# Attention with mixed heads and routed experts: scores of two pairs of heads per visit, one visit for all products with v, neighbouring columns in the second mixing

## The chip, the core and the metric

The kernel runs on one core of one Trainium2 chip. The metric is the device time of one execution in microseconds (us). A core has five engines that work at the same time, each through its own instructions in a fixed order: TensorE (PE, matrix products, with weight loads listed as PEld), VectorE (DVE), ScalarE (ACT), GpSimd (POOL) and SyncE (SP, which here only issues transfers). They wait for one another through semaphores. PE writes its results to PSUM, a small memory of eight banks per partition, and DVE or ACT copy them out to the main on-chip memory.

## What is computed

Attention over 8 batches, 12 heads, 448 positions and 64 values per head, with two mixings of the heads (before and after the softmax), and then a layer of 8 experts of which each row uses one:

```python
scores = scale * np.matmul(q, k.transpose(0, 1, 3, 2))
scores = np.einsum('bhij,hg->bgij', scores, w_pre)
scores = scores - np.max(scores, axis=-1, keepdims=True)
attn = np.exp(scores)
attn = attn / (np.sum(attn, axis=-1, keepdims=True) + 1e-09)
attn = np.einsum('bhij,hg->bgij', attn, w_post)
x = np.matmul(attn, v)                      # then heads side by side: 3584 x 768
...
logits = x @ w_gate
expert_idx = np.argmax(logits, axis=1)
...
for e in range(E):
    h = np.maximum(xe @ w1[e], 0.0)
    out[mask] = gate_w[mask, None] * (h @ w2[e])
```

All data are float32.

## The kernel before

The attention works on 32 tiles T: four to a batch, three of 120 queries and one of 88 (`it` is the tile's number in its batch). The 12 heads are 6 pairs c; a pair's two heads lie in the two halves of the partitions.

For each tile, `qk` (L203) is called once per pair. It makes the scores of the pair with six matrix products, three for each head (q and k are split into a high and a low part, and high x high, high x low and low x high are added). The two heads use the upper and the lower half of the array's rows at the same time and write two PSUM banks, the tile `bs` (bank_s). ACT then copies both banks to `si` (L215). There is one such pair of banks, so the next visit waits until ACT has emptied it. I call one call of `qk` a **scores visit**.

SP's transfers (`relayout`, L227) then gather 10 queries x 12 heads onto partitions, into one of four `sb` tiles. Such a **block** holds two groups of at most 10 queries; a tile of 120 has 6 blocks, the tile of 88 has 5, the last of them with one group. Group n of N holds the queries n, n+N, n+2N, ... (`queries`, L61). For every block stand one after the other:

- `mix` (L234), the **first mixing**: a product of full array width per group (L241, into `bm`; a float32 product is run as two passes, which the profile lists as two MATMUL), the negative maximum on DVE (L242), the exponential with its sum on ACT (L243).
- `weigh` (L248): one over the sum on DVE (L251, L253), and the mixing weights scaled by it, `wp`, on POOL (L256).
- `post` (L260), the **second mixing**, one step later: four products of full width per group (L267, into `bp`), which also turn the block so that keys lie on partitions; DVE copies them to `pt` (L271). Since a group's queries lie N apart, this copy writes every N-th column of `pt` (N is 12, or 9 in the short tile).

When all blocks of a tile are done, `av` (L278), the **products with v**, runs in two halves g of three pairs: 24 products each (L286), the two heads of a pair side by side in two halves of the array's columns, into one bank `ba`; DVE copies it to `xt` (L289). `rows` (L293) turns the result back into rows and multiplies by the router's weights, in two parts (L301, into a bank `bx`; ACT L303, DVE L304). `dispatch` (L313) finds each row's expert and place: small DVE rows, two tiny products (L328, L329, into `bx`), and an indirect transfer that POOL issues (L346).

`split_q` (L115) makes the high and the low part of q, on ACT (L121) and POOL (L122).

What runs when is a list of steps u, one for each block: `at(u, priority, what)` in L386 to L407 puts a call into a step, and within a step calls go by priority. Scores of a tile were spread over the steps from 8 to 4 ahead of its first block, the second mixing stands one step behind its first mixing, and the products with v, the rows and the dispatch some steps behind the tile's last block. A scheduler then sets the final order on each engine, so that it may differ from the list by some places; on the chip every engine keeps this order.

Behind the attention comes the expert stage (from L421), which the change doesn't touch.

Of the kernel before, what the change touches and what calls it, by code (L numbers as in the profile page):

```python
# [23 lines left out]
P = 128  # L24
IT = 120
# [15 lines left out]
def attn_moe_kernel(ctx, tc, qT, kT, v, w_pre, w_post, w_gate, w1, w2, out):  # L41
# [19 lines left out]
    def queries(T, s, c):  # L61
        N, n = geom[T][4], 2 * s + c
        return slice(n, n + N * (geom[T][3][s][c] - 1) + 1, N)

# [16 lines left out]
    ps_a = att.enter_context(tc.tile_pool(name="ps_a", bufs=1, space=PSUM))  # L81
    ps_x = att.enter_context(tc.tile_pool(name="ps_x", bufs=1, space=PSUM))

    bank_s = ps_s.tile([P, 2, 512], F32, name="bs")
    bank_m = [ps_m.tile([P, 512], F32, name=f"bm{n}") for n in range(2)]
    bank_p = [ps_p.tile([JC, 512], F32, name=f"bp{n}") for n in range(2)]
    bank_a = ps_a.tile([P, 3, IT], F32, name="ba")
    bank_x = [ps_x.tile([P, 512], F32, name="bx"), bank_s[:, 0, :]]
# [26 lines left out]
    def split_q(T, part):  # L115
        ni = geom[T][2]
        if part == 0:
# [3 lines left out]
        nc.scalar.copy(out=qh[:, cs, :ni], in_=QR[T][:, cs, :ni])  # L121
        nc.gpsimd.tensor_sub(out=ql[:, cs, :ni], in0=QR[T][:, cs, :ni],  # L122
                             in1=qh[:, cs, :ni].bitcast(F32))
# [79 lines left out]
    def qk(T, c):  # L203
        b, it, ni = geom[T][:3]
        if c == 0:
            SI[T] = si_p.tile([IT, H, S], F32, name="si")
        kh, kl = KK[b, c]
        qh, ql = QQ[T]

        for n, (qx, kx) in enumerate(((qh, kh), (qh, kl), (ql, kh))):  # L210
            for r in range(2):
                hs = slice(r * D, (r + 1) * D)
                nc.tensor.matmul(out=bank_s[:ni, r, :S], lhsT=qx[hs, c, :ni], rhs=kx[hs, :],  # L213
                                 start=(n == 0), stop=(n == 2))
        nc.scalar.copy(out=SI[T][:ni, 2 * c:2 * c + 2, :], in_=bank_s[:ni, :, :S])  # L215
        m = (it - 2) * NPAIR + c - NPAIR + 2
        if b + 1 < B:
            if 0 <= m < NPAIR:
                load_k(b + 1, m)
            if 1 <= m <= NPAIR:  # L220
                split_k(b + 1, m - 1)
# [5 lines left out]
    def relayout(T, s):  # L227
        sb = sbs[nsb["n"] % len(sbs)]
        nsb["n"] += 1
        for c, nq in enumerate(geom[T][3][s]):  # L230
            nc.sync.dma_start(out=sb[R0:R0 + nq * H, c, :], in_=SI[T][queries(T, s, c)])
# [43 lines left out]
    PA = {}  # L275


    def av(T, g):  # L278
        b, it, ni = geom[T][:3]
        if g == 0:  # L280
            XT[T] = x_p.tile([P, NPAIR, IT], F32, name="xt")
        for p in range(3):
            for c in range(NJ):
                for r in range(2):
# [390 lines left out]
```

## Time and profile before

| what | value |
|---|---|
| time, median of 3 runs | 1592.8 us (1588.83 to 1593.34) |
| the profiled execution | 1589.2 us |
| its span, first to last instruction | 1587.0 us |
| PE: busy, share of the span | 1511.4 us, 95% |
| DVE, ACT, POOL: share of the span | 56%, 42%, 27% |

The profile shows one execution. Its page lists groups of instructions by source line, with how often they ran, their busy time and the mean duration of one. The trace behind the page answers further questions: the busy time of each engine in a stretch of time, who waited for whom, and the instructions of an engine in the order of time. In such a timeline a row has the start (us from the span's beginning), the time until the last of the row's instructions ended, the engine, the line, the operation, output<-inputs, their shapes, and how many instructions were merged. Since PE overlaps the end of one product with the start of the next, the distance from start to start tells what an instruction costs, and the busy time doesn't.

PE starts in the attention at 7.5 us and with the expert stage at 1026 us.

### The profile page before, as it was taken

Reading aid. Unit: us, or ns where it says so; the run is one execution under the profiler, and the core shown is the slowest. Engines: PE = TensorE matmul, PEld = TensorE weight load, DVE = VectorE, ACT = ScalarE, POOL = GpSimd, SP = SyncE. Lnnn points to the kernel's source line nnn. Section 1 sums busy time; section 2 is a strip of 40 time slices with the busy share of each in tenths; the row PEclk is TensorE's granted clock in tenths of the full one; section 3 lists DMA queues with packets and bytes.
Section 4 is the critical chain, followed back from the end, with each engine's and each line's share of the span. In section 5 each row is a group of like instructions: output and inputs, shape, how many; then the busy total and the mean of one; then the engine's idle time right before and its main releaser. Section 6 shows DMA issues by size and latency. Waiting matters only on the chain. (4 is left out here: it accounts for less than half of the span.)

```text
span 1587.0 us, 29453 instructions
## 1 busy us (share of the span) xinstructions
PE 1511.4 (95%) x11056; PEld 1190.4 (75%) x11056; DVE 892.5 (56%) x2003; ACT 661.5 (42%) x1424; POOL 429.8 (27%) x595
## 2 busy tenths in 40 slices
PE   5999999999999999999999999499999999999996
PEld 2767777777777767777777776498988898997986
DVE  1666767767766776776776768435243333434320
ACT  4554454454454454554445444134233222333320
POOL 5443342342352342343233222112012020201100
PEclk9999999999999999999999999799999999999998
DMA  7443343342443433433423224345162433426210
GB/s 204 138 135 107 128 143 107 125 151 97 137 137 101 149 124 108 150 118 118 143 102 112 88 98 138 97 134 198 40 226 84 155 136 103 162 84 216 97 50 37
DMA packets 114465, 197.51 MB, mean 124 GB/s; under 512 B 39746, under 2 KB 88914, under 8 KB 114308
## 3 DMA queue, kind: packets, MB, share of 16 engines
q1 hardware_dynamic: 107200, 171.51, 33.4%
q0 software_dynamic: 6064, 23.86, 4.1%
q8 instruction: 100, 1.64, 0.4%
q14 instruction: 57, 0.47, 0.1%
q10 hardware_dynamic: 1044, 0.04, 0.0%
HBM read 96.01 MB, written 23.06 MB: 75 GB/s over the span
## 5 line engine op out<-in xcount | busy, mean ns | idle before, releaser
L243 ACT ACTIVATE et<-bm,st 124x448 f32<-124x448 f32 x360 | 225.7, 631 | 424.1 <-DVE st L242 332.8
L271 DVE COPY pt<-bp 112x480 f32<-112x480 f32 x360 | 344.3, 1011 | 47.8 <-PE bp L267 47.1
L256 POOL TENSOR_SCALAR wp<-Wpost,st 124x120 f32<-124x120 f32 x360 | 208.1, 589 | 566.5 <-DVE st L253 531.3
L267 PEld LDWEIGHTS bp<-wp,et 124*112 124x112 f32 x2880 | 309.5, 177 | 60.3 <-issue 51.8
L267 PE MATMUL bp<-wp,et 124*112 124x120 f32 x2880 | 345.8, 272 | 4.6 <-POOL wp L256 3.9
L241 PE MATMUL bm<-sb,Wpre 124*124 124x448 f32 x720 | 305.4, 546 | 0.0
L242 DVE TENSOR_REDUCE st<-bm 124x1 f32<-124x448 f32 x360 | 218.4, 614 | 25.1 <-PE bm L241 17.1
L215 ACT COPY si<-bs 120x896 f32<-120x896 f32 (+1 forms) x192 | 172.7, 899 | 33.1 <-PE bs L213 33.0
L286 PEld LDWEIGHTS ba<-pt,vt 112*64 112x64 f32 x3072 | 151.7, 138 | 32.3 <-issue 22.1
L241 PEld LDWEIGHTS bm<-sb,Wpre 124*124 124x124 f32 x720 | 120.8, 187 | 68.4 <-issue 62.5
L286 PE MATMUL ba<-pt,vt 112*64 112x120 f32 (+1 forms) x3072 | 169.0, 263 | 1.5 <-DVE m L320 1.0
L531 POOL DMA_INDIRECT out<-y,ti x30 | 33.4, 1113 | 464.2 <-ACT xh L458 338.4
L503 PE MATMUL pm_h<-xh,ah 128*128 128x512 f32 (+1 forms) x384 | 148.1, 386 | 1.9 <-ACTq L555 0.7
L503 PE MATMUL pm_h<-xl,ah 128*128 128x512 f32 (+1 forms) x384 | 147.5, 384 | 0.0
L503 PE MATMUL pm_h<-xh,al 128*128 128x512 f32 (+1 forms) x384 | 147.4, 384 | 0.0
L213 PEld LDWEIGHTS bs<-kh,qh 64*120 64x120 f32 (+1 forms) x384 | 34.0, 174 | 135.6 <-issue 98.2
L522 PE MATMUL pm_y<-bh,hh 128*128 128x384 f32 x480 | 127.9, 343 | 0.0
L522 PE MATMUL pm_y<-bl,hh 128*128 128x384 f32 x480 | 123.6, 336 | 0.0
L507 DVE SCALAR_TENSOR_TENSOR hl<-pm_h,hh 128x512 fp32r<-128x512 f32 (+1 forms) x64 | 42.1, 657 | 141.2 <-ACT hh L506 141.2
L522 PE MATMUL pm_y<-bh,hl 128*128 128x384 f32 x480 | 121.1, 336 | 0.0
L213 PE MATMUL bs<-kh,qh 64*120 64x448 f32 (+1 forms) x384 | 90.4, 467 | 24.0 <-ACT si L215 15.1
L527 DVE TENSOR_SCALAR y<-pm_y,tb 128x384 f32<-128x384 f32 x30 | 18.4, 614 | 159.9 <-PE pm_y L522 159.9
(102 smaller groups left out, 1756.2 us busy)
## 6 DMA issues: line engine op xcount, KB each, us to landing
sb<-si SPq DMA_DIRECT2D x344, 210.0 KB
wraw<-in_w SPq DMA_DIRECT2D x48, 512.0 KB
wraw<-in_w SPq DMA_DIRECT2D x64, 384.0 KB
kr<-in_kT SPq DMA_DIRECT2D x48, 224.0 KB
vt<-in_v SPq DMA_DIRECT2D x8, 1344.0 KB
qr<-in_qT SPq DMA_DIRECT2D x48, 180.0 KB
XD<-xr SPq DMA_DIRECT2D x24, 360.0 KB
sb<-si SPq DMA_DIRECT2D x16, 189.0 KB
```

Of the source, the lines that this page charges most:

```text
L213: nc.tensor.matmul(out=bank_s[:ni, r, :S], lhsT=qx[hs, c, :ni], rhs=kx[hs, :], start=(n == 0), stop=(n == 2))
L215: nc.scalar.copy(out=SI[T][:ni, 2 * c:2 * c + 2, :], in_=bank_s[:ni, :, :S])
L241: nc.tensor.matmul(out=bm, lhsT=Wpre[:R1, :], rhs=sb[:R1, c, :], start=True, stop=True)
L242: nc.vector.reduce_max(out=st[:R1, 0, c:c + 1], in_=bm, axis=AX.X, negate=True)
L243: nc.scalar.activation(out=et[:R1, c, :], in_=bm, func=AF.Exp, bias=st[:R1, 0, c:c + 1], scale=1.0, accum_out=st[:R1, 1, c:c + 1])
L256: nc.gpsimd.tensor_scalar(out=wp[:R1, c, :], in0=Wpost[:R1], scalar1=st[:R1, 2, c:c + 1], scalar2=None, op0=ALU.mult)
L267: nc.tensor.matmul(out=pp[:, c * IT:(c + 1) * IT], lhsT=et[:R1, n, c * JC:(c + 1) * JC], rhs=wp[:R1, n, :], start=True, stop=True)
L271: nc.vector.tensor_copy(out=PT[T][:, :, :, queries(T, s, n)].rearrange("p c h i -> p (c h) i"), in_=bank_p[n][:, :NJ * IT].rearrange("p (x ...
L286: nc.tensor.matmul(out=bank_a[r * D:(r + 1) * D, p, :ni], lhsT=VV[b][:, c, h * D:(h + 1) * D], rhs=PT[T][:, c, h, :ni], start=(c == 0), st ...
L503: nc.tensor.matmul(out=ph[:, :n], lhsT=wx[:, fs], rhs=xx[:, kt, :n], start=(m == 0), stop=(m == 3 * NK1 - 1))
L507: nc.vector.scalar_tensor_tensor(out=hl[:, ft, :n], in0=ph[:, :n], scalar=0.0, in1=hh[:, ft, :n].bitcast(F32), op0=ALU.max, op1=ALU.subtract)
L522: nc.tensor.matmul(out=py[g][:, :384], lhsT=hx[:, kt, ts], rhs=wx[:, g * 384:(g + 1) * 384], start=(n == 0), stop=(n == 3 * NK2 - 1))
```

## The change

Five things are changed, all of them in the attention.

1. **Scores of two pairs per visit.** `qk(T, g)` makes pairs 2g and 2g + 1, one into each of two pairs of banks (`bank_s` is now a list of two tiles of two banks); then ACT copies both. Visits stand at the steps 8, 6 and 4 ahead of the tile's first block (7, 5, 3 for the first tile of a batch and 7, 6, 4 for the second: `QSTEP`).
2. **All products with v in one visit.** `av(T)` makes both halves, one in the first bank of each of the two score tiles; the two copies stand behind.
3. **The banks `ba` and `bx` are gone.** `rows` writes the first bank of the one and of the other score tile, `dispatch` the second bank of the first. So these four banks serve the scores, the products with v, the row projection and the dispatch in turn.
4. **Neighbouring columns.** `queries` now gives a group a run of neighbouring columns of `pt`. To match, `split_q` writes the queries of q in another order, so that rows n, n+N, ... of the scores hold neighbouring queries; `relayout` reads the same stepped rows as before (`parts`). The stepped access is thus in `split_q`'s outputs, no longer in the copy to `pt`. The short tile's split takes two instructions each where one did, since its groups have two sizes.
5. **Steps of the tail.** `rows` (both parts) stands w = 2 steps behind `av`, `dispatch` 2 further, all with priority 6, behind the first and ahead of the second mixing of the step; before, the halves of `av` and `rows` were spread over the next tile.

```diff
-    def queries(T, s, c):
+    def parts(T, s, c):
         N, n = geom[T][4], 2 * s + c
         return slice(n, n + N * (geom[T][3][s][c] - 1) + 1, N)
+
+    def queries(T, s, c):
+        nq = sum(geom[T][3], [])
+        i0 = sum(nq[:2 * s + c])
+        return slice(i0, i0 + nq[2 * s + c])
...
-    bank_s = ps_s.tile([P, 2, 512], F32, name="bs")
+    bank_s = [ps_s.tile([P, 2, 512], F32, name=f"bs{n}") for n in range(2)]
...
-    bank_a = ps_a.tile([P, 3, IT], F32, name="ba")
-    bank_x = [ps_x.tile([P, 512], F32, name="bx"), bank_s[:, 0, :]]
...
-        nc.scalar.copy(out=qh[:, cs, :ni], in_=QR[T][:, cs, :ni])
-        nc.gpsimd.tensor_sub(out=ql[:, cs, :ni], in0=QR[T][:, cs, :ni],
-                             in1=qh[:, cs, :ni].bitcast(F32))
+        i0 = 0
+        for k in sorted(set(nq), reverse=True):
+            n0, n1 = nq.index(k), nq.index(k) + nq.count(k)
+            src = QR[T][:, cs, i0:i0 + k * (n1 - n0)].rearrange("p c (n i) -> p c n i", i=k)
+            hi, lo = (q[:, cs, :N * k].rearrange("p c (i n) -> p c n i", n=N)[:, :, n0:n1, :]
+                      for q in (qh, ql))
+            nc.scalar.copy(out=hi, in_=src)
+            nc.gpsimd.tensor_sub(out=lo, in0=src, in1=hi.bitcast(F32))
+            i0 += k * (n1 - n0)
...
+        for c in (2 * g, 2 * g + 1):
+            kh, kl = KK[b, c]
+            for n, (qx, kx) in enumerate(((qh, kh), (qh, kl), (ql, kh))):
+                for r in range(2):
+                    hs = slice(r * D, (r + 1) * D)
+                    nc.tensor.matmul(out=bank_s[c % 2][:ni, r, :S], lhsT=qx[hs, c, :ni],
+                                     rhs=kx[hs, :], start=(n == 0), stop=(n == 2))
+        for c in (2 * g, 2 * g + 1):
+            nc.scalar.copy(out=SI[T][:ni, 2 * c:2 * c + 2, :], in_=bank_s[c % 2][:ni, :, :S])
...
+        for g in range(2):
+            pa = bank_s[g][:, 0, :3 * IT].rearrange("p (c i) -> p c i", i=IT)
+            for p in range(3):
+                for c in range(NJ):
+                    for r in range(2):
+                        h = 2 * (3 * g + p) + r
+                        nc.tensor.matmul(out=pa[r * D:(r + 1) * D, p, :ni],
...
-        px = bank_x[part] if T == NTILE - 1 else bank_x[0]
+        px = bank_s[part][:, 0, :]
...
-        pr = bank_x[0]
+        pr = bank_s[0][:, 1, :]
...
+    QSTEP = {0: (7, 5, 3), 1: (7, 6, 4)}
...
-        for c in range(NPAIR):
-            at(max(u0 - QLEAD + c * 5 // 6, -1), 3, qk, T, c)
+        for g in range(3):
+            at(max(u0 - QSTEP.get(it, (8, 6, 4))[g], -1), 3, qk, T, g)
...
-        w = len(geom[T + 1][3]) - 1 if T + 1 < NTILE else 0
-        for g in range(2):
-            at(ua + g * w // 2, 6, av, T, g)
-            at(ua + g * w // 2 + 1, 9, rows, T, g)
-        at(ua + w // 2 + 2, 9, dispatch, T)
+        w = 2 if T + 1 < NTILE else 1
+        at(ua, 6, av, T)
+        for part in range(2):
+            at(ua + w, 6, rows, T, part)
+        at(ua + 2 * w, 6, dispatch, T)
```

How this changes the order on PE shows in two places. The rows below give line, operation, output<-inputs (bm, bp: banks of the first and second mixing; ba, bs, bx: of products with v, scores, rows), shape, and how many alike follow each other. In the changed kernel the lines are L225 for the scores, L255 and L281 for the mixings, L299 for the products with v, L316 for the rows, L343 and L344 for the dispatch; bs_101 and bs_102 are the two score tiles.

The first place is on PE in the first batch, where a tile of 120 queries gets its products with v. Before:

```order
L241 MATMUL bm_109<-sb_181,Wpre 124x448
L213 MATMUL bs<-kh,qh 120x448 x2
L213 MATMUL bs<-kl,qh 120x448 x2
L213 MATMUL bs<-kh,ql 120x448 x2
L286 MATMUL ba<-pt,vt 64x120 x9
L213 MATMUL bs<-kh,qh 120x448 x2
L213 MATMUL bs<-kl,qh 120x448 x2
L213 MATMUL bs<-kh,ql 120x448 x2
L286 MATMUL ba<-pt,vt 64x120 x15
L267 MATMUL bp_110<-wp,et 112x120 x4
L267 MATMUL bp_111<-wp,et 112x120 x4
```

A scores visit stands ahead of the half of the products with v, and another one within it. In the changed kernel, on PE in such steps, there is one stretch of products with v, and a scores visit in the step behind it:

```order
L255 MATMUL bm_104<-sb_176,Wpre 124x448
L299 MATMUL bs_101<-pt,vt 64x120 x24
L299 MATMUL bs_102<-pt,vt 64x120 x24
L281 MATMUL bp_105<-wp,et 112x120 x4
L281 MATMUL bp_106<-wp,et 112x120 x4
L255 MATMUL bm_103<-sb_173,Wpre 124x448
L255 MATMUL bm_104<-sb_173,Wpre 124x448
```

Two halves and the scores between them have become one run of 48, with full-width mixings on both sides.

The second place is on PE around a dispatch at the boundary of the first two batches, behind the one-group block of the short tile. Before:

```order
L241 MATMUL bm_109<-sb_183,Wpre 124x448
L213 MATMUL bs<-kh,qh 120x448 x2
L213 MATMUL bs<-kl,qh 120x448 x2
L213 MATMUL bs<-kh,ql 120x448 x2
L267 MATMUL bp_110<-wp,et 112x120 x4
L328 LDWEIGHTS tri
L328 MATMUL bx<-ohb,tri 120x8
L329 LDWEIGHTS ones
L329 MATMUL bx<-ohb,ones 128x8
L241 MATMUL bm_108<-sb_180,Wpre 124x448
```

In the changed kernel, on PE at that boundary:

```order
L255 MATMUL bm_104<-sb_176,Wpre 124x448
L225 MATMUL bs_101<-kh,qh 120x448 x2
L225 MATMUL bs_101<-kl,qh 120x448 x2
L225 MATMUL bs_101<-kh,ql 120x448 x2
L225 MATMUL bs_102<-kh,qh 120x448 x2
L225 MATMUL bs_102<-kl,qh 120x448 x2
L225 MATMUL bs_102<-kh,ql 120x448 x2
L343 LDWEIGHTS tri
L343 MATMUL bs_101<-ohb,tri 120x8
L344 LDWEIGHTS ones
L344 MATMUL bs_101<-ohb,ones 128x8
L281 MATMUL bp_105<-wp,et 112x120 x4
```

The dispatch's products have moved from behind the second mixing to straight behind the scores, and write the tile bs_101, which those scores have just filled and which ACT copies out.

More of the change, by code (lines that the diff above doesn't have):

```diff
@@ L80, in attn_moe_kernel @@
     ps_p = att.enter_context(tc.tile_pool(name="ps_p", bufs=1, space=PSUM))
-    ps_a = att.enter_context(tc.tile_pool(name="ps_a", bufs=1, space=PSUM))
-    ps_x = att.enter_context(tc.tile_pool(name="ps_x", bufs=1, space=PSUM))
-    bank_s = ps_s.tile([P, 2, 512], F32, name="bs")
+    bank_s = [ps_s.tile([P, 2, 512], F32, name=f"bs{n}") for n in range(2)]
     bank_m = [ps_m.tile([P, 512], F32, name=f"bm{n}") for n in range(2)]
     bank_p = [ps_p.tile([JC, 512], F32, name=f"bp{n}") for n in range(2)]
-    bank_a = ps_a.tile([P, 3, IT], F32, name="ba")
-    bank_x = [ps_x.tile([P, 512], F32, name="bx"), bank_s[:, 0, :]]
     KR, KK, QR, QQ, VV, SI, SB, EE, PT, XT = ({} for _ in range(10))
@@ L115, in split_q @@
     def split_q(T, part):
-        ni = geom[T][2]
+        N = geom[T][4]
+        nq = sum(geom[T][3], [])
         if part == 0:
@@ L200, in attn_moe_kernel, with qk @@
                         in_=none.unsqueeze(1).to_broadcast([P, 8, ROWS // P // 8, 2]))
-    def qk(T, c):
+    def qk(T, g):
         b, it, ni = geom[T][:3]
-        if c == 0:
+        if g == 0:
             SI[T] = si_p.tile([IT, H, S], F32, name="si")
-        kh, kl = KK[b, c]
         qh, ql = QQ[T]
[L210 to L221, printed above, removed]
+        for c in (2 * g, 2 * g + 1):
[7 more added lines that the diff above has]
+            nc.scalar.copy(out=SI[T][:ni, 2 * c:2 * c + 2, :], in_=bank_s[c % 2][:ni, :, :S])
+            m = (it - 2) * NPAIR + c - NPAIR + 2
+            if b + 1 < B:
+                if 0 <= m < NPAIR:
+                    load_k(b + 1, m)
+                if 1 <= m <= NPAIR:
+                    split_k(b + 1, m - 1)
     nsb = {"n": 0}
@@ L230, in relayout @@
         for c, nq in enumerate(geom[T][3][s]):
-            nc.sync.dma_start(out=sb[R0:R0 + nq * H, c, :], in_=SI[T][queries(T, s, c)])
+            nc.sync.dma_start(out=sb[R0:R0 + nq * H, c, :], in_=SI[T][parts(T, s, c)])
         SB[T, s] = sb
@@ L273, in post, with av @@
                 in_=bank_p[n][:, :NJ * IT].rearrange("p (x i) -> p x i", i=IB)[:, :, :nq])
-    PA = {}
-    def av(T, g):
+    def av(T):
         b, it, ni = geom[T][:3]
[L280 to L284, printed above, removed]
-                    h = 2 * (3 * g + p) + r
-                    nc.tensor.matmul(out=bank_a[r * D:(r + 1) * D, p, :ni],
-                                     lhsT=VV[b][:, c, h * D:(h + 1) * D],
-                                     rhs=PT[T][:, c, h, :ni], start=(c == 0), stop=(c == NJ - 1))
-        nc.vector.tensor_copy(out=XT[T][:, 3 * g:3 * g + 3, :ni], in_=bank_a[:, :, :ni])
+        XT[T] = x_p.tile([P, NPAIR, IT], F32, name="xt")
+        for g in range(2):
[5 more added lines that the diff above has]
+                        nc.tensor.matmul(out=pa[r * D:(r + 1) * D, p, :ni],
+                                         lhsT=VV[b][:, c, h * D:(h + 1) * D],
+                                         rhs=PT[T][:, c, h, :ni], start=(c == 0), stop=(c == NJ - 1))
+        for g in range(2):
+            pa = bank_s[g][:, 0, :3 * IT].rearrange("p (c i) -> p c i", i=IT)
+            nc.vector.tensor_copy(out=XT[T][:, 3 * g:3 * g + 3, :ni], in_=pa[:, :, :ni])
     XR, LG = {}, {}
```

## The prediction

> **What bounds the kernel now.** First the page's top line, then the windows view for the attention stage (stretch, length, busy time and instructions of PE, PEld, DVE, ACT, POOL, then granted clock, DMA share, GB/s), then the two longest of PE's waits in that stage (sum, times, longest).
>
> ```profile
> span 1587.0 us, 29453 instructions
> 40.00:1000.00 960.00, 949.11 (x8078) 686.70 (x8074) 678.83 (x1661) 471.43 (x1122) 334.73 (x488) 1.00 0.38 122
> PE bs L213 <- ACT si L215: 4.8, 15, 0.6
> PE bp L267 <- POOL wp L256: 3.9, 3, 1.8
> ```
>
> Between 40 and 1000 us PE is busy for 949.1 of 960.0 us at the full granted clock, and its two longest waits come to 8.7 us in all. DVE has 71% of that stretch and ACT 49%. So PE's own row of instructions is the clock of this stage; the change doesn't touch the expert stage behind it. A saving must therefore come out of the distance from start to start on PE. Busy time doesn't show that, because a fill or a drain counts as busy. So I read PE's timeline (start, duration, instruction, count).
>
> ```profile
> 479.06 1.67 PE L241 MATMUL bm<-sb,Wpre 124*124 124x448 f32 x4
> 480.66 0.46 PE L213 MATMUL bs<-kh,qh 64*120 64x448 f32 x2
> 480.96 0.36 PE L213 MATMUL bs<-kl,qh 64*120 64x448 f32 x2
> 481.16 0.36 PE L213 MATMUL bs<-kh,ql 64*120 64x448 f32 x2
> 481.45 1.90 PE L267 MATMUL bp<-wp,et 124*112 124x120 f32 x16
> 483.18 0.86 PE L301 MATMUL bx<-xg,xt 128*120 128x136 f32 x6
> ...
> 985.03 1.67 PE L241 MATMUL bm<-sb,Wpre 124*124 124x448 f32 x4
> 986.54 1.80 PE L267 MATMUL bp<-wp,et 124*112 124x120 f32 x16
> 988.18 0.86 PE L301 MATMUL bx<-xg,xt 128*120 128x136 f32 x6
> ```
>
> The two stretches hold the same first and second mixing (L241, L267), once with a scores visit (L213) between them and once without. L241 takes 1.60 us to the scores (479.06 to 480.66), but 1.51 us straight to L267. L267 takes 1.73 us behind the scores, 1.64 us without them. Inside the visit one step is 0.20 us (480.96 to 481.16), while the whole visit takes 0.79 us where three such steps would be 0.60. Going from full-width products to half-array products and back thus costs 0.09 in front, 0.19 inside and 0.09 behind: **0.37 us for a visit that stands alone**, whatever it computes.
>
> The products with v (L286) have the same kind of price, and are dearer where a scores visit cuts a half in two:
>
> ```profile
> 494.68 2.68 PE L286 MATMUL ba<-pt,vt 112*64 112x120 f32 x48
> 494.94 2.42 PE L286 MATMUL ba<-pt,vt 112*64 112x120 f32 x44
> 497.09 0.27 PE L286 MATMUL ba<-pt,vt 112*64 112x120 f32 x2
> 497.29 1.89 PE L267 MATMUL bp<-wp,et 124*112 124x120 f32 x16
> ...
> 505.28 1.24 PE L286 MATMUL ba<-pt,vt 112*64 112x120 f32 x18
> 506.81 0.47 PE L213 MATMUL bs<-kh,qh 64*120 64x448 f32 x2 [0.29 <-ACT si L215]
> 507.61 1.85 PE L286 MATMUL ba<-pt,vt 112*64 112x120 f32 x30
> 509.40 1.89 PE L267 MATMUL bp<-wp,et 124*112 124x120 f32 x16
> ```
>
> The rows with 44 and with 2 are the same visit, seen from later: 42 instructions in 2.15 us are 0.0512 each. Then 48 would take 2.46 us; the visit takes 2.61 (494.68 to 497.29), 0.15 of its own, plus the 0.09 behind it. The half that was cut takes 1.53 + 1.79 = 3.32 us beside the scores visit in it, 0.71 more. Second mixings are cut too:
>
> ```profile
> 415.51 1.48 PE L267 MATMUL bp<-wp,et 124*112 124x120 f32 x12
> 417.08 0.47 PE L213 MATMUL bs<-kh,qh 64*120 64x448 f32 x2
> 417.88 0.67 PE L267 MATMUL bp<-wp,et 124*112 124x120 f32 x4
> 418.38 0.86 PE L301 MATMUL bx<-xg,xt 128*88 128x136 f32 x6
> ```
>
> Its parts take 1.57 and 0.50 us, 2.07 against 1.73: 0.34 more.
>
> **The change, part by part.** How often each case stands there is counted in the order of PE's instructions, of which the section on the change shows two places.
>
> *Visits, before.* Of 192 scores visits nine stand at the very start. 108 stand alone (0.37 each, 40.0 us); 44 stand right ahead of products with v and share the way back (0.09 + 0.19 = 0.28, 12.3 us); 17 cut a second mixing (0.34 + 0.19 = 0.53, 9.0 us); 14 cut a half of the products (0.71 + 0.19 = 0.90, 12.6 us). Of 64 halves 62 have their own 0.15 and 0.09 (14.9 us), and 18 also an entry from full width (1.6 us). Sum: 90.4 us.
>
> *Visits, after.* 90 scores visits of two pairs stand alone (six are at the start) and none cuts anything: 90 x 0.37 = 33.3 us. The step from the first pair to the second, in other banks, occurs nowhere in this trace. It lies between 0.20, a step within a visit, and 0.30, the first step (480.66 to 480.96). I take 0.20, since at that point the array stays in its halves; 0.30 would add 96 x 0.10 = 9.6 us. 32 visits of the products cost 0.09 + 0.15 + 0.09 = 0.33, 10.6 us. Sum 43.9, so **this part saves 46.5 us**. Matrix work, row projection and dispatch have the same instructions as before.
>
> *Neighbouring columns.* The copy out of the second mixing writes every twelfth column, and is slow for its size beside a copy of neighbouring columns:
>
> ```profile
> L271 DVE COPY pt<-bp 112x480 f32<-112x480 f32 x360 | 344.3, 1011 | 47.8 <-PE bp L267 47.1
> 497.41 0.53 DVE L289 COPY xt<-ba 128x360 f32<-128x360 f32 x1 [1.22 <-PE ba L286]
> ```
>
> By the second row's pace 480 elements would take some 0.65 to 0.70 us. That frees about 0.33 x 360 = 119 us on DVE, and I cost it at **nothing**: DVE is idle for 29% of the stage and PE hardly waits for it. If the copies stayed at 1.01 us, nothing would be lost against this sum either. The stepped columns move to the split of q, on ACT and POOL, whose pieces may grow by as much; both engines are idle for over half of the stage, so this too is nothing, unless it comes between ACT's two copies out of the score banks (below).
>
> *Start.* Until 31 us most scores visits wait for ACT to empty the only pair of banks:
>
> ```profile
> 10.90 0.73 PE L213 MATMUL bs<-kh,qh 64*120 64x448 f32 x2 [1.00 <-ACT si L215]
> 29.29 0.73 PE L213 MATMUL bs<-kh,qh 64*120 64x448 f32 x2 [1.00 <-ACT si L215]
> ```
>
> These are the first and the last of six such waits of 1.00 us. A second pair of banks takes them away, but the low parts of k and q, made one after the other on POOL, are late next. I take 2.5 us, with 0 and 6 as bounds.
>
> *End.* For the last tile nothing is left to lie beside:
>
> ```profile
> 1000.78 1.00 PE L286 MATMUL ba<-pt,vt 112*64 112x88 f32 x14 [1.01 <-DVE m L320]
> 1005.35 2.04 PE L286 MATMUL ba<-pt,vt 112*64 112x88 f32 x48 [0.53 <-DVE xt L289]
> 1007.33 0.93 PE L301 MATMUL bx<-xg,xt 128*88 128x136 f32 x6
> 1008.09 0.86 PE L301 MATMUL bs<-xg,xt 128*88 128x136 f32 x6
> ```
>
> From the first product with v to the last row projection it is 7.31 us, with a wait for the one bank. Two halves in two banks take about 3.8 us (twice the 1.98 from 1005.35 to 1007.33, less one 0.15), then the second copy and its handing over about 0.65: 4.45 us, **2.8 us less**.
>
> *The added wait.* Scores, products with v, row projection and dispatch now share four banks. At ordinary places 3.2 us of second and first mixing lie between a scores visit and the next user. At one place at each of the seven boundaries of batches the dispatch (L343 in the changed kernel) stands straight behind a scores visit and writes a bank that ACT has yet to empty; everything on PE is queued behind it. ACT's pace behind a first mixing:
>
> ```profile
> 502.87 1.67 PE L241 MATMUL bm<-sb,Wpre 124*124 124x448 f32 x4
> 505.24 0.63 ACT L243 ACTIVATE et<-bm,st 124x448 f32<-124x448 f32 x1
> 505.86 0.90 ACT L215 COPY si<-bs 120x896 f32<-120x896 f32 x1
> 506.56 1.15 POOL L256 TENSOR_SCALAR wp<-Wpost,st 124x120 f32<-124x120 f32 x2 [2.42 <-DVE st L253]
> ```
>
> The copy starts 2.99 us behind the start of L241 and ends at 3.89. PE reaches the dispatch after 1.60 + 1.39 (0.79 and three steps) = 2.99. So it waits 0.9, and some 0.4 more since DVE there has a copy to pt in front of the maxima: 1.3 us, seven times, **9.1 us lost**. Bounds: 0, if ACT came early, and 2.2 each (the second copy waited for too), 15.4.
>
> *Sum.* 46.5 + 2.5 + 2.8 - 9.1 = 42.7. The span goes from 1587.0 to 1544.3; the profiled execution took 1589.2 with 2.2 around the span, so 1546.5. That execution lies 3.6 below the median of the runs (1592.8, from 1588.83 to 1593.34), which would give 1550.1. I take the middle, **1548 us**.
>
> **Rivals.**
>
> *The reciprocal's chain is late behind a dispatch.* The second mixing needs wp, which comes from L241 by way of DVE, ACT, DVE and POOL: 4.84 us after the start of L241 for both halves (502.87 to 506.56 + 1.15), 4.26 for the first. In a dispatch step, now without scores, DVE has dispatch's small rows and a copy to pt in front of the reciprocal, and POOL has this in front of wp:
>
> ```profile
> L346 POOL DMA_INDIRECT TB<-tg,di x30 | 31.5, 1048 | 62.5 <-DVE tg L339 59.5 <-DVE st L251 3.0
> ```
>
> So the first half is ready at about 4.26 + 1.05 + 0.65 + 0.2 = 6.2 us. PE comes to it after 1.51 + 1.64 + 1.60 + 1.39 = 6.14. That is just even; 0.5 us late at 31 dispatches would add 15: 1563 us. For it speaks the cover, which is gone; against it, that PE waited for wp only three times so far.
>
> *Evacuation sets the pace.* Two copies out of the score banks take 1.80 us on ACT (0.90 each), the visit that fills them 1.39. If PE paid that difference at every visit, 96 x 0.41 = 39 us, the time would be 1587 us. The Trainium skill (TensorEngine Tiling (Array Packing), section PSUM Bottleneck) states such a rule: array tiling speeds up the products but not the emptying of PSUM, and both ScalarE and VectorE should do it; here ScalarE does it alone. By that rule 1587 us, by the rows 1548; the trace so far agrees only at the start, where visits follow each other. In the steady part 3.2 us of other work lie between.
>
> *Slower: the wait of the seven places comes at every visit.* ACT works in order, and its copies stand behind both exponentials, which stand behind DVE's maxima. At an ordinary place the first copy ends 3.89 us after L241 starts, and the next user of the bank comes at 2.99 + 1.73 + 1.51 = 6.23. If ACT were over 2.34 us late there, because maxima stand behind pt copies that wait for PE, the banks would be missed at the other 83 visits too. At 1.3 us each that is 108 us: 1656 us. It turns the sign from 0.5 us a visit. Against it: ACT idles for half of the stage.
>
> *Step between pairs at 0.30:* 1558 us. *Dispatch finds its bank free* (no wait at the seven places, all of the start's six microseconds): 1548 - 9 - 3.5 = 1536 us. *The change doesn't do what it says:* if full-width and half-array stretches cost the same wherever they stand, only start, end and the seven waits remain, +3.8 us: 1597 us; the two stretches above speak against it.
>
> **How the numbers follow.** Chances: the forecast 0.52, the late reciprocal 0.13, the free dispatch 0.12, the dearer step 0.10, evacuation 0.05, slower 0.05, nothing gained 0.03. The range goes from 1535 to 1573: down to the free dispatch, and up by the dearer step (10) and the late reciprocal (15) together. Outside it are the last three, 0.13. About 0.3% is what a measurement of this kernel can tell from no change, 1588 to 1597.6 us: faster than that are the first four, 0.87; within it, evacuation and nothing gained, 0.08; slower 0.05.
>
> **What would show it.** In the changed kernel's PE timeline: a scores visit of 1.39 us between 1.60 and 1.73 (1.49 if the step is 0.30); about 5.08 us for the products with v of a full tile; seven waits of 0.9 to 1.7 us in the dispatch for the copies out of the score banks, and next to no other wait that names ACT, DVE or POOL. The copy to pt should stand at 0.65 to 0.70 us with PE's time unmoved by it. The forecast is wrong if second mixings wait for wp, if first mixings wait for the exponentials, or if the pairs' step is dear.

## The result and the profile after

The changed kernel takes 1555.52 us (median of 4 runs, 1554.32 to 1558.43) against 1592.55 us before: a ratio of 0.978, with a 95% interval of 0.976 to 0.979. Its profiled execution took 1554.7 us, with a span of 1552.8. First the page's top line, the attention stage in the windows view (columns as in the prediction), and what PE waited for there:

```profile
span 1552.8 us, 29553 instructions
40.00:960.00 920.00, 906.90 (x8063) 692.44 (x8061) 590.81 (x1673) 481.85 (x1138) 349.56 (x505) 1.00 0.40 128
PE bp L281 <- POOL wp L270: 6.9, 6, 2.4
PE bs L343 <- ACT si L228: 6.0, 7, 0.9
L285 DVE COPY pt<-bp 112x480 f32<-112x480 f32 x360 | 234.8, 652 | 87.5 <-PE bp L281 85.6
```

PE's row of instructions is still the clock: it is busy for 906.9 of 920 us. The seven waits in the dispatch (L343) are there, 0.9 us each at most. The waits for wp are 6.9 us in sum where they were 3.9 before; all six lie behind 926 us, in the last two tiles, where no scores are left to stand in between. The copy to pt (L285, from the page's groups) has gone from 1011 to 652 ns. PE's timeline shows the visits:

```profile
476.97 1.67 PE L255 MATMUL bm<-sb,Wpre 124*124 124x448 f32 x4
478.58 0.46 PE L225 MATMUL bs<-kh,qh 64*120 64x448 f32 x2
...
479.99 1.90 PE L281 MATMUL bp<-wp,et 124*112 124x120 f32 x16
...
490.26 1.67 PE L255 MATMUL bm<-sb,Wpre 124*124 124x448 f32 x4
491.87 0.47 PE L225 MATMUL bs<-kh,qh 64*120 64x448 f32 x2
...
494.21 0.17 PE L343 MATMUL bs<-ohb,tri 120*120 120x8 bf16 x1 [0.85 <-ACT si L228]
...
586.80 5.14 PE L299 MATMUL bs<-pt,vt 112*64 112x120 f32 x96
591.87 1.90 PE L281 MATMUL bp<-wp,et 124*112 124x120 f32 x16
```

A first mixing still takes 1.61 us to the scores. The visit of two pairs takes 1.41 (478.58 to 479.99), the products with v of a full tile 5.07. The dispatch comes 2.34 us after its scores visit began and waits 0.85 of that for ACT. The expert stage begins at 982.5 us; before it began at 1026.2. So the attention stage is **43.7 us** shorter. The expert stage before, in the windows view, and PE's wait for the gathered rows there:

```profile
1026.20:1587.00 560.80, 532.94 (x2784) 485.64 (x2784) 200.41 (x274) 169.12 (x264) 67.53 (x58) 0.97 0.35 123
PE pm_x L456 <- DMA xs<-XD,tcl: 24.3, 7, 15.1
```

The same two rows after:

```profile
982.50:1552.80 570.30, 536.31 (x2784) 488.38 (x2784) 200.36 (x274) 169.02 (x264) 68.18 (x58) 0.97 0.34 121
PE pm_x L473 <- DMA xs<-XD,tcl: 28.3, 7, 14.5
```

The expert stage, in which nothing was changed, takes **9.5 us longer**, with the same number of instructions on every engine. That is the part of the expected gain that is missing. The first of the seven waits is the start of the stage; the other six come to 9.2 us before and 13.8 after. One of them on PE's timeline after, and then the windows view of three stretches after:

```profile
1109.68 0.51 PE L539 MATMUL pm_y<-bh,hl 128*128 128x384 f32 x2
1112.88 1.51 PE L473 MATMUL pm_x<-ident,xs 128*128 128x128 f32 x6 [2.69 <-DMA xs<-XD,tcl]
1114.05 0.99 PE L539 MATMUL pm_y<-bh,hh 128*128 128x384 f32 x2
...
1112.60:1116.00 3.40, 3.12 (x12) 3.15 (x13) 1.22 (x1) 1.50 (x2) 1.41 (x1) 0.51 1.02 408
1331.10:1334.50 3.40, 3.40 (x13) 3.40 (x14) 1.23 (x1) 0.86 (x2) 1.41 (x1) 0.50 1.01 396
1395.90:1402.80 6.90, 4.97 (x14) 3.94 (x15) 2.23 (x3) 3.21 (x5) 1.41 (x1) 0.51 0.99 361
```

And the one such stretch before:

```profile
1093.40:1096.90 3.50, 3.50 (x10) 2.70 (x9) 1.31 (x2) 1.66 (x2) 0.83 (x1) 0.51 1.02 402
```

At the three longest of the six waits after (2.69, 2.85 and 3.12 us) the granted clock falls to a half (column behind POOL) for 3.4 or 6.9 us, 13.7 us in all; before it falls once, for 3.5 us, behind a wait of 1.61 us. Half of the difference, 5.1 us, is lost, and with 4.6 of longer waits this makes 9.7, about the 9.5 us. So the question for the experiments was, beside the terms of the sum, why the same gathers land later. The trace offers one difference. One of the DMA queues (q8) brings instructions in transfers of 16 KB. In the attention stage there are 67 of them both before and after, one for every 256 rows on PE's queue; in the expert stage they come closer together, 33 for 5651 rows. The attention stage of the changed kernel has 45 more rows on PE's queue (17173 against 17128 up to the first pm_x, bare waits among them), so in the expert stage the transfers stand at other places. The DMA queues (packets, MB, share of the engines) while the fifth of the six gathers runs, from its issue to its landing, after:

```profile
q1 hardware_dynamic: 454, 1.51, 56.2%
q0 software_dynamic: 249, 1.24, 40.5%
q8 instruction: 1, 0.02, 0.8%
q14 instruction: 1, 0.01, 0.2%
```

and before:

```profile
q1 hardware_dynamic: 381, 1.29, 57.1%
q0 software_dynamic: 188, 0.96, 41.8%
q14 instruction: 1, 0.01, 0.3%
```

After, one 16 KB transfer (q8) falls into it; before, none does. A smaller transfer on another instruction queue (q14) falls into it in both.

### The profile page after: what moved, and what is told of

It reads as the page before. It is cut to its first block, busy times and chain, and to the rows that moved or that the text cites. A ratio compares the mean times of both kernels' runs of the same rounds, so it can differ in the third digit from the quotient of the medians.

```text
span 1552.8 us, 29553 instructions
## 1 busy us (share of the span) xinstructions
PE 1472.4 (95%) x11056; PEld 1198.8 (77%) x11056; DVE 802.7 (52%) x2003; ACT 674.5 (43%) x1440; POOL 444.1 (29%) x611
## 5 line engine op out<-in xcount | busy, mean ns | idle before, releaser
L281 PE MATMUL bp<-wp,et 124*112 124x120 f32 x2880 | 338.6, 270 | 7.2 <-POOL wp L270 7.2
L281 PEld LDWEIGHTS bp<-wp,et 124*112 124x112 f32 x2880 | 308.7, 177 | 42.7 <-issue 24.4
L255 PE MATMUL bm<-sb,Wpre 124*124 124x448 f32 x720 | 302.2, 541 | 0.1
L285 DVE COPY pt<-bp 112x480 f32<-112x480 f32 x360 | 234.8, 652 | 87.5 <-PE bp L281 85.6
L256 DVE TENSOR_REDUCE st<-bm 124x1 f32<-124x448 f32 x360 | 224.6, 624 | 49.2 <-PE bm L255 37.6
L255 PEld LDWEIGHTS bm<-sb,Wpre 124*124 124x124 f32 x720 | 119.8, 187 | 68.1 <-issue 63.3
L228 ACT COPY si<-bs 120x896 f32<-120x896 f32 (+1 forms) x192 | 169.5, 910 | 6.2 <-PE bs L225 6.0
L299 PEld LDWEIGHTS bs<-pt,vt 112*64 112x64 f32 x3072 | 147.4, 137 | 21.2 <-issue 15.1
L299 PE MATMUL bs<-pt,vt 112*64 112x120 f32 (+1 forms) x3072 | 154.3, 260 | 0.7 <-DVE pt L285 0.7
L523 ACT ACTIVATE hh<-pm_h 128x512 fp32r<-128x512 f32 (+1 forms) x64 | 36.6, 571 | 158.2 <-PE pm_h L520 157.9
L225 PEld LDWEIGHTS bs<-kh,qh 64*120 64x120 f32 (+1 forms) x384 | 35.4, 174 | 80.7 <-issue 26.2
```

Of the source, the lines that this page charges most:

```text
L255: nc.tensor.matmul(out=bm, lhsT=Wpre[:R1, :], rhs=sb[:R1, c, :], start=True, stop=True)
L256: nc.vector.reduce_max(out=st[:R1, 0, c:c + 1], in_=bm, axis=AX.X, negate=True)
L281: nc.tensor.matmul(out=pp[:, c * IT:(c + 1) * IT], lhsT=et[:R1, n, c * JC:(c + 1) * JC], rhs=wp[:R1, n, :], start=True, stop=True)
L285: nc.vector.tensor_copy(out=PT[T][:, :, :, queries(T, s, n)].rearrange("p c h i -> p (c h) i"), in_=bank_p[n][:, :NJ * IT].rearrange("p (x ...
L299: nc.tensor.matmul(out=pa[r * D:(r + 1) * D, p, :ni], lhsT=VV[b][:, c, h * D:(h + 1) * D], rhs=PT[T][:, c, h, :ni], start=(c == 0), stop=( ...
L523: nc.scalar.activation(out=hh[:, ft, :n], in_=ph[:, :n], func=AF.Relu)
```

## The experiments

**Stepped columns put back.** `queries` is `parts` again and `split_q` copies whole pieces:

```
-        nq = sum(geom[T][3], [])
-        i0 = sum(nq[:2 * s + c])
-        return slice(i0, i0 + nq[2 * s + c])
+    queries = parts
```

> The changed kernel with one part undone: the copy to pt writes every twelfth column again and the split of q has whole pieces. Theory (PE's row sets the pace, DVE is covered): the copy to pt goes back from 0.65 to about 1.01 us and DVE from 56% to about 71% of the attention stage, but that stage stays within 1 us of the changed kernel's, time 1553 to 1559 us. Rival (neighbouring columns carry part of the gain, since DVE's copies stand in front of the reciprocal): second mixings wait for wp behind the 31 dispatches, 0.36 us or more each, 1566 us or more. On the expert stage, which took 570.3 us in the changed kernel and 560.8 before with the same instructions: if what runs before it decides its length, it is 569 to 572 here; if it varies from one execution to the next, anything from 560 to 572.

1560.27 us (1559.2 to 1564.52), ratio to before 0.9816 (0.9791 to 0.9841). Up to the last first mixing it is as the theory has it, since DVE's load goes up and PE's row doesn't notice; that mixing starts at 954.5 us in both. The copy, the same stretch of the attention stage, and two rows at the end, of this kernel:

```profile
L274 DVE COPY pt<-bp 112x480 f32<-112x480 f32 x360 | 345.4, 1011 | 43.2 <-PE bp L270 41.0
40.00:960.00 920.00, 905.19 (x8045) 690.65 (x8043) 663.40 (x1670) 464.04 (x1120) 334.22 (x487) 1.00 0.41 128
960.10 1.17 PE L270 MATMUL bp<-wp,et 124*112 124x120 f32 x8 [2.38 <-POOL wp L259]
962.28 6.49 PE L288 MATMUL bs<-pt,vt 112*64 112x88 f32 x96 [1.01 <-DVE pt L274]
```

The attention stage still ends 4.5 us later (987.0) and not within 1 us, and the time lies above the theory's 1559; all of that comes in the last tile, where DVE is in the chain: longer waits for wp and pt, and then the products with v at half clock (6.49 us where the changed kernel takes 3.86). The kernel with a spare tile, further down, fell into half clock at the same place with neighbouring columns, so how much of the 4.5 us the columns decide isn't settled. The expert stage was 570.1 us, as in the change.

**Neighbouring columns alone, in the kernel before.** The edit is the opposite one, in the kernel before.

> The kernel before with neighbouring columns alone (copy to pt and split of q as in the change, nothing else). Theory: copy to pt 0.65 us, time as before, 1589 to 1596 us. Rival (the copy's length reaches PE): at least 5 us faster, 1587 or less. Expert stage: 560 to 562 us if what runs before it decides its length, anything from 560 to 572 if it varies from one execution to the next.

1592.22 us (1588.03 to 1594.29), ratio 1.0008 (0.9992 to 1.0024): no difference, though the copy took 653 ns here too. The theory holds; the columns are worth nothing while PE's row has the pace. The expert stage took 564.0 us, 3.2 more than before and outside the 560 to 562 expected of a stage that doesn't vary from one execution to the next.

**The dispatch in another bank.**

```
-        pr = bank_s[0][:, 1, :]
+        pr = bank_m[0][:, S:]
```

> The changed kernel, but the dispatch's two products go to the 64 columns that the first mixing leaves free in its first bank, not into a score bank. Theory (the seven waits in the dispatch are for ACT to empty the bank): they go, and the attention stage is 6.0 to 6.6 us shorter, time 1548 to 1551 us. Rival (the dispatch is also late for DVE's small rows, 0.4 us of my 1.3): the waits stay at 0.4 or more each and name DVE, 3 us gained, 1552 us or more. A third way: the first mixing now waits for DVE to have read the dispatch's columns, and the gain is given back.

1575.99 us (1572.83 to 1579.27), ratio 0.9906 (0.9883 to 0.993): 20 us slower than the change, and the theory missed. PE's waits, PE's timeline around a dispatch, and two rows of DVE and POOL there:

```profile
PE bp L281 <- POOL wp L270: 19.0, 24, 2.4
...
524.75 1.67 PE L255 MATMUL bm<-sb,Wpre 124*124 124x448 f32 x4
526.26 0.98 PE L281 MATMUL bp<-wp,et 124*112 124x120 f32 x8
527.27 0.17 PE L343 MATMUL bm<-ohb,tri 88*88 88x8 bf16 x1
...
529.89 0.15 DVE L267 RECIPROCAL st<-st 124x2 f32<-124x2 f32 x1
530.27 1.04 POOL L361 DMA_INDIRECT TB<-tg,di  x1 [5.43 <-DVE st L267]
532.00 1.89 PE L281 MATMUL bp<-wp,et 124*112 124x120 f32 x16 [0.67 <-POOL wp L270]
```

The waits for ACT's copies are gone, but the dispatch now shares a tile with the first mixing. It has to let the exponential finish, so it stands in the middle of a second mixing (527.27, 2.52 us after L255; 1.51 in the changed kernel). The reciprocal follows the dispatch's small rows, POOL issues the transfer ahead of wp, and the next second mixing waits. This is the rival of the late reciprocal, 24 times: the two steps take 3.51 and 5.47 us there, where the changed kernel takes 3.27 and 4.74. The change itself escapes it because its dispatch comes early in the step.

**One pair per visit.** `qk` handles one pair, at the steps of before:

```
-        for g in range(3):
-            at(max(u0 - QSTEP.get(it, (8, 6, 4))[g], -1), 3, qk, T, g)
+        for c in range(NPAIR):
+            at(max(u0 - QLEAD + c * 5 // 6, -1), 3, qk, T, c)
```

> The changed kernel with one pair of heads per scores visit at the steps of before, on the two pairs of banks in turn; products with v, row projection and dispatch as in the change. Theory (a visit costs 0.37 us whatever it computes): 90 more visits, 90 x 0.37 = 33 us slower than the changed kernel, less 0.09 for those that stand right ahead of products with v and less a few us where the dispatch finds its bank free: 1580 to 1590 us. Rival (the gain came from more banks and from whole products, not from fewer visits): within 8 us of the changed kernel.

1595.71 us (1589.11 to 1603.17), ratio 1.0032 (1.0011 to 1.0053): the whole gain is gone, and more than the 1580 to 1590 allowed for. The attention stage ends at 1027.1 us, 44.6 later. My 90 was a miscount, though: pairs 0 and 1 share a step, and PE's timeline has 149 visits, 59 more than the change. At 0.37, less 0.09 for the 30 ahead of products with v, these cost 19.1 us. Another part is of another kind:

```profile
PE bs L316 <- ACT si L228: 11.9, 14, 0.9
PE bs L299 <- ACT si L228: 7.0, 23, 0.6
```

With a visit in nearly every step, the row projection and the products with v come straight behind scores and wait for the same banks: 19.2 us in all against 6.0 in the change. Some 12 us remain, where row projections and dispatches now cut second mixings; they weren't taken apart. So the rival is out, fewer visits carry the gain; but they carry it in two ways, by the price of a visit and by leaving steps in which the shared banks come free.

**Products with v in two visits.** `av` takes the half as an argument:

```
-        at(ua, 6, av, T)
+        at(ua, 6, av, T, 0)
+        at(ua, 7.5, av, T, 1)
```

> The changed kernel with the products with v in two visits again, half of them ahead of the second mixing and half behind, in the same banks. Theory (each visit of them costs 0.15 of its own and 0.09 on either side, whatever it computes): 32 x 0.33 = 10.6 us slower in the attention stage, 993 us to the expert stage where the changed kernel takes 982.5, time 1563 to 1569 us. Rival (one visit or two is the same, and only the scores visits count): within 3 us of the changed kernel.

1563.22 us (1558.77 to 1564.59), ratio 0.9815 (0.9792 to 0.9838). The two visits on PE's timeline:

```profile
475.03 2.68 PE L300 MATMUL bs<-pt,vt 112*64 112x120 f32 x48
477.64 1.89 PE L281 MATMUL bp<-wp,et 124*112 124x120 f32 x16
479.47 2.68 PE L300 MATMUL bs<-pt,vt 112*64 112x120 f32 x48
482.08 1.77 PE L255 MATMUL bm<-sb,Wpre 124*124 124x448 f32 x4
```

Twice 2.61 us, 0.15 more than the one visit's 5.07, and the wider steps around them. The attention stage ends at 995.1 us, 12.6 later against 10.6 expected. In 3.4 us of it, from 948 us on, the granted clock is a half while PE is busy throughout, which is 1.7 us that the changed kernel doesn't lose there; without them it is 10.9. So the price of a visit is shown, and to size.

**The place of the instruction transfers.** Four kernels have products of one number by one number at the start, where PE waits for its first data anyway. They write a corner of a bank that the first mixing overwrites:

```
+    pad = const.tile([1, 2], BF16, name="pad")
+    nc.vector.memset(pad, 0.0)
+    for _ in range(106):
+        nc.tensor.matmul(out=bank_m[0][:1, :1], lhsT=pad[:, 0:1], rhs=pad[:, 1:2], start=True, stop=True)
```

In the changed kernel 106:

> The changed kernel with 106 products of one number by one number (two instructions each) ahead of everything on PE, where it waits 7.85 us for the first data. Nothing else is changed. What they move is the place in PE's program at which the queue of instruction transfers brings the next 16 KB (every 256 instructions of PE in the traces so far). In the expert stage of the changed kernel one such transfer starts between 1.0 us ahead of and 3.7 us behind the issue of the gather of xs, at five of the experts; before it was 10 to 11 us behind. The attention stage of the changed kernel has 45 more instructions on PE's queue than before; 212 more make 257, one round of 256 and one. Theory (this transfer delays the gather that PE waits for, and the longer wait then halves the granted clock): the transfers stand 10 to 11 us behind the gather again, expert stage back from 570 to 561 to 566 us, time 1546 to 1551 us, if the products at the start cost nothing. Rival (the expert stage is longer for another reason that comes from the attention stage, or varies by execution): transfers moved, expert stage still 569 to 572 us.

1545.63 us (1539.87 to 1553.03), ratio 0.9717 (0.9688 to 0.9745), expert stage 556.5 us. PE's wait for the gather:

```profile
PE pm_x L477 <- DMA xs<-XD,tcl: 23.4, 7, 14.5
```

And 128:

> As the kernel with 106 such products, but 128: 256 instructions, a full round, so the 16 KB transfers stand where they stand in the changed kernel. Theory of the transfers: expert stage 569 to 572 us, as in the changed kernel. Rival (the extra products themselves, or the moved start, make the expert stage shorter): the same length as with 106.

1553.0 us (1552.22 to 1557.92), ratio 0.9765 (0.9743 to 0.9786), expert stage 567.1 us:

```profile
PE pm_x L477 <- DMA xs<-XD,tcl: 31.1, 7, 14.2
```

In the kernel before, 22 of them:

> The kernel before with 22 such products at the start: 44 instructions more on PE's queue, so the 16 KB transfers stand where the changed kernel has them. Theory of the transfers: the expert stage grows from 560.8 (564.0 with neighbouring columns) to 568 to 572 us, with nothing of the change in it, and the time to 1597 to 1602 us. Rival (the attention stage of the change is what lengthens it): 560 to 565 us, time as before.

1593.02 us (1588.84 to 1597.77), ratio 1.0014 (0.9996 to 1.0032). The same wait:

```profile
PE pm_x L460 <- DMA xs<-XD,tcl: 28.6, 7, 14.7
```

Without the first, 8.9, 16.9 and 13.9 us: short with 106, long with 128, which differs from it only in the number of products, and long in the kernel before once 22 had moved its transfers. But all three stages are shorter than expected: 556.5 us (561 to 566 expected), 567.1 (569 to 572) and, in the kernel before, 562.6 (568 to 572). What these kernels have beside the products is a tile more, so everything behind it lies 32 bytes further. One kernel has that alone.

```
+    spare = const.tile([1, 2], BF16, name="spare")
+    nc.vector.memset(spare, 0.0)
```

> The changed kernel with one spare tile of 32 bytes a partition ahead of the others, nothing else: what the kernels with products at the start have beside these. In those the products of the expert stage with 512 columns (L520 of the changed kernel) follow each other in 0.2267 us, not 0.2333. Theory (the address does that, apart from the 16 KB transfers): 0.2267 us here too, while the transfers stay where the changed kernel has them and the gathers are waited for as long as there: expert stage 562 to 567 us, time about 1549 us. Rival (the products at the start do it): 0.2333 us, expert stage 569 to 573 us, time 1553 to 1558 us.

1549.98 us (1544.16 to 1559.27), ratio 0.9735 (0.9712 to 0.9758). The windows view of 25 us of the expert stage's first products alone (PE, PEld), in the changed kernel:

```profile
1270.00:1295.00 25.00, 25.00 (x109) 20.13 (x108) 1.00 0.48 162
```

and in this one:

```profile
1276.00:1301.00 25.00, 25.00 (x112) 20.68 (x112) 1.00 0.47 158
```

The same products at the same granted clock, 112 in the time of 109. A run of 144 takes 32.64 us, not 33.59, and six experts have such a run: 5.7 us. The address does it, not the products at the start. Its profiled execution was the slowest of its five, which lie 15 us apart, and its expert stage, 569.0 us, lies above the range I gave. So the kernel before with 22 products had gained by the address what it lost by the transfers. Its control, with 128:

> The kernel before with 128 products at the start: addresses as in the kernel before with 22, but a full round of 256 instructions, so the 16 KB transfers stand 10 to 11 us behind the gather as before. Theory (transfers and addresses apart): waits ahead of pm_x behind the first of 9 to 10 us in sum against 13.9 with 22 products, expert stage 554 to 559 us against 562.7, time 1585 to 1589 us. Rival (the place of the transfers does not matter in the program of before): 561 to 564 us and 1592 to 1594 us, as with 22.

1587.35 us (1583.21 to 1590.67), ratio 0.9979 (0.9965 to 0.9994), expert stage 558.9 us, six waits 10.0 us. As expected of the transfers, and 5.7 us below the kernel with 22.

**The dispatch one step later.**

```
-        at(ua + 2 * w, 6, dispatch, T)
+        at(ua + 2 * w + (it == 2), 6, dispatch, T)
```

> The changed kernel with the dispatch of each batch's third tile one step later, where it stands ahead of the products with v of the fourth and not behind a scores visit. Theory: the seven waits of 0.85 to 0.94 us for ACT's copies go and nothing takes their place, since 3.2 us of mixing lie between the scores visit and the dispatch, and 3.8 us of products behind it cover the reciprocal's chain: attention stage 6.0 to 6.6 us shorter than the changed kernel's 982.5. Rival (the dispatch is late for DVE, or wp is late behind it, as in the kernel with the dispatch in the first mixing's bank): 3 us or less gained, or a loss.

1548.29 us (1543.79 to 1553.44), ratio 0.9721 (0.9702 to 0.9739). PE there:

```profile
491.98 1.67 PE L255 MATMUL bm<-sb,Wpre 124*124 124x448 f32 x4
493.49 0.17 PE L343 MATMUL bs<-ohb,tri 120*120 120x8 bf16 x1
...
493.62 4.00 PE L299 MATMUL bs<-pt,vt 112*64 112x88 f32 x96
```

The seven waits are gone and nothing stands in their place there. The last first mixing starts at 949.5 us, 5.0 earlier, behind one new wait of 1.0 us for an exponential at 922.6; the expert stage starts at 979.1, 3.4 earlier, since 1.6 us went to half clock in the last tile. So less than the 6.0 expected came through.

**All three together**: the later dispatch, and 95 products at the start, for the address and for the place of the transfers.

> The changed kernel with the dispatch of each third tile one step later, and 95 products at the start, which with that order of PE put the 16 KB transfers where they were before. Theory: the three gains add up. Attention stage 979 us as with the later dispatch, or up to 3 us more by the start; expert stage 555 to 561 us as with 106 products; time 1538 to 1545 us, the fastest so far. Rival (the later dispatch gains nothing by itself): 1546 to 1550 us.

**1542.58 us** (1535.95 to 1543.02), ratio 0.969 (0.966 to 0.971), the fastest of all. Attention stage 979.0 us, expert stage 559.0 us, six waits of 10.9 us.

All kernels by the place of the transfer that comes nearest to each of the six gathers, worked out from the trace's packets:

| kernel | behind the gather's issue, us | six waits, us | expert stage, us |
|---|---|---|---|
| before | 9.9 to 11.1 | 9.2 | 560.8 |
| before, neighbouring columns | 10.3 to 10.8 | 9.4 | 564.0 |
| one pair per visit | 9.9 to 11.5 | 9.9 | 566.3 |
| products with v in two visits | 10.4 to 11.3 | 11.7 | 567.6 |
| 106 products (moved 32 bytes) | 9.9 to 10.7 | 8.9 | 556.5 |
| before, 128 (moved 32 bytes) | 10.2 to 10.9 | 10.0 | 558.9 |
| all three (moved 32 bytes) | 10.4 to 11.1 | 10.9 | 559.0 |
| the change | -1.5 to 3.7 | 13.8 | 570.3 |
| stepped columns | -1.4 to 3.4 | 13.8 | 570.1 |
| dispatch in another bank | -0.8 to 3.7 | 14.9 | 573.1 |
| dispatch later | -2.8 to -1.0 | 13.4 | 572.6 |
| 128 products (moved 32 bytes) | -2.2 to 3.3 | 16.9 | 567.1 |
| before, 22 (moved 32 bytes) | -1.5 to 3.4 | 13.9 | 562.6 |
| moved 32 bytes alone | -1.5 to 3.4 | 14.0 | 569.0 |

The two groups don't overlap in the waits. Among kernels at the same addresses the stage is 6.8 us longer on average with the transfer near the gather (571.5 against 564.7), and 8.1 among those moved by 32 bytes (566.2 against 558.1). Within such a group it still varies by 2.5 to 7 us from kernel to kernel. Each row is one profiled execution, but on each of the three chips of the experiments both groups occur, with the longer waits in the same one, and the medians over all executions agree: 128 products are 7.4 us slower than 106, and 22 in the kernel before 5.7 slower than 128.

The single gathers show it more sharply. From its issue to PE's product a gather takes 6.1 to 7.5 us, 6.6 on average, in the 42 cases with the transfer 10 us behind; 6.1 to 7.6, 7.0 on average, in the 29 where the transfer starts between 2.8 us ahead of the issue and 0.3 behind; and 7.4 to 8.2, 7.9 on average, in the 13 where it starts 2.0 to 3.7 us behind, while the gather runs. PE's wait is 1.7, 2.1 and 3.0 us on average. So the longest waits go with a transfer inside the gather; in the change these are the last two, which give 2.9 of the 4.6 us.

The kept traces also tell when the clock falls. In all of them it changes only on a grid of 3.41 us. Take the windows of this grid from 35 us on in which PE has the full clock, in all fourteen traces, and add up PE's idle time in each. With 1.92 us or more the next window was at half clock in 64 of 64 cases; with 1.63 to 1.91 us in 14 of 30; with 1.0 to 1.62 us in none of 68. So the longer a wait is, the likelier its window goes past that bound; the wait of 1.61 us before stood in a window with 1.83 us of idle time.

## Why the prediction was right, and where it was off

The forecast was 1548 us with 1535 to 1573 around it, and the sum for the profiled execution 1546.5; it took 1554.7, 8.2 more. Point by point:

- **Visits, 46.5 us saved.** From the second first mixing (35.37 us before, 33.60 after) to the last (994.82 and 954.50) PE takes 38.6 us less. With the 6.0 us that it waits in the dispatch and 2.0 more than before for wp added back, this is 46.6. The parts are on the timeline: visits of 1.41 us (1.39 forecast), products of 5.07 (5.08), the step between pairs at 0.20 to 0.21. Taking the visits apart again costs what the price says for the products with v; for the scores it costs the price and, beyond it, waits for the shared banks that the sum had no place for, since the change doesn't have them.
- **The added wait, 9.1 us.** The seven waits came at the forecast places for the forecast reason, 6.0 us in all. The 0.4 us each that I added because DVE has a copy to pt in front of the maxima didn't exist: ACT begins its copy 3.00 us behind the first mixing's start there (490.26 to 493.26), where the sum without that delay has 2.99.
- **Start, 2.5 us.** Not there at the first mixing, which starts at 31.1 us (30.7 before): the waits for the banks are gone, but PE waits for ACT's high parts instead (3.32 us at 16.9, 1.71 at 25.6). The second first mixing starts 1.8 us earlier, for a reason that the sum didn't have: the first one takes 1.69 us instead of 3.28.
- **End, 2.8 us.** From the first product with v of the last tile to the end of the last row projection 5.41 us against 8.17 before: 2.8. The size is luck in part. Before, the granted clock was 0.51 from 1001.20 to 1004.70 us, with PE busy throughout, which the prediction didn't see; that is 1.7 of the 2.8, and the changed kernel's profiled execution has no such stretch there, while some of the other kernels have one.
- **Neighbouring columns, nothing.** The copy took 652 ns (0.65 to 0.70 forecast). Alone, in the kernel before, they gained nothing. In the last tile they may count, which the sum left out.
- **The rivals.** Emptying at the pace of PSUM and the wait at every visit didn't occur in the change. The late reciprocal didn't either as long as there were scores; in the last two tiles second mixings waited for wp six times, 3.0 us more than before, for which the sum had no term. It cost 19.0 us of waits as soon as the dispatch was moved to a worse place in its step, so it was near. The emptying rule of the Trainium skill (TensorEngine Tiling (Array Packing), section PSUM Bottleneck) doesn't decide here: ACT alone empties every visit and PE waits 6.0 us in all.

Attention together: 42.7 forecast, 43.7 measured. That these lie 1.0 us apart is luck in part: the added wait came out 3.1 us smaller, against which stand the waits for wp and the smaller start. **The step that failed** is one sentence of the first part: "the change doesn't touch the expert stage behind it". Its instructions are untouched, but it begins at another place of PE's program, the instruction transfers fall beside or into the gathers, PE waits 4.6 us longer for those and the clock halves more often: 9.5 us, more than the whole difference from the sum. That the place of the transfers lengthens the waits is shown by the pairs that differ only in it and in the number of products at the start (106 and 128; 22 and 128 before): in the first the kernel with more products waits longer, in the second the one with fewer. That the longer waits make the clock fall is borne out by the count of windows above. How one 16 KB transfer keeps a gather back, at a time when the DMA engines are full (share 0.99 to 1.02 above), stays open.

## What to carry to other kernels

Price a switch between array modes by pitch on PE's timeline, from start to start, with and without the visit; then count the visits in the order of instructions. Where users share PSUM banks, look for the step in which one stands straight behind the filling of its bank: that is where the new wait will be, and moving the light one by a step removes it. A stage that a change doesn't touch can still move by 0.6% of the kernel's time when the number of instructions ahead of it or the addresses change, so compare it by itself, and use a control that changes those alone.

## What the hardware showed beyond that

- In the attention stage one 16 KB instruction transfer comes for every 256 rows on PE's queue (67 for 17173). Near a gather that PE waits for, such transfers go with waits of 13.4 to 16.9 us in sum instead of 8.9 to 11.7.
- Products of 128 rows by 512 columns follow each other in 0.2267 us instead of 0.2333 when the tiles lie 32 bytes further, at the same granted clock. Which of the operands matters wasn't tried.
- Behind PE's longer waits for a gather the granted clock falls to 0.5 for 3.4 us, or 6.9, also where PE waited for only 2.69 us (at 1112.88). The Trainium skill (TensorE: Matmul & The Clock Gate, Part 1: The HAM clock gate) has the clock halved after at least one idle window of about 3.4 us. The length of the stretches agrees with that window (3.40 us), the condition doesn't: 1.92 us of idle time within one window of 3.41 us were enough in all 64 cases. With stepped columns put back, half clock in the last tile of the attention made the products with v 6.49 us long instead of 3.86.
- 106 products of one number by one number took 2.78 us on an idle PE.
